# A gated linear attention with a mixture of experts on one core: the opening in another order, the attention's transfers spread over its steps, and the last 64 tokens of an expert in one load of weights

## The chip, the cores and the metric

The kernel runs on one core of one Trainium2 chip. The time is the device time of one execution in microseconds (us). The core has five engines with a queue of instructions each: PE (matrix products; its loads of the stationary operand are listed apart as PEld), DVE (vector work), ACT (activations and copies), POOL (vector work and indirect transfers) and SP, which here only issues transfers. Every engine works its queue in order; semaphores make it wait for the others. Transfers run beside the engines on 16 DMA engines.

## The reference

Two stages follow each other. The first is a gated linear attention for 4 batches, 8 heads, 768 positions and 40 dimensions, whose gates are kept in range by a running maximum `m`; the second sends each of the 3072 rows (4 x 768) of 320 values to one of 8 experts.

```python
for t in range(S):
    kt, vt, qt = (k[:, :, t], v[:, :, t], q[:, :, t])
    m_new = np.maximum(f_gate[:, :, t] + m, i_gate[:, :, t])
    f_stab = np.exp(f_gate[:, :, t] + m - m_new)
    i_stab = np.exp(i_gate[:, :, t] - m_new)
    m = m_new
    C = f_stab[:, :, None, None] * C + i_stab[:, :, None, None] * np.einsum('bhd,bhe->bhde', vt, kt)
    n = f_stab[:, :, None] * n + i_stab[:, :, None] * kt
    h_tilde = np.einsum('bhde,bhe->bhd', C, qt)
    nq = np.einsum('bhd,bhd->bh', n, qt)[:, :, None]
    denom = np.maximum(np.abs(nq), 1.0)
    o = 1.0 / (1.0 + np.exp(-o_gate[:, :, t]))
    y[:, :, t] = o * h_tilde / denom
...
xn = x / (np.linalg.norm(x, axis=-1, keepdims=True) + 1e-06)
en = expert_emb / (np.linalg.norm(expert_emb, axis=-1, keepdims=True) + 1e-06)
logits = xn @ en.T / tau
expert_idx = np.argmax(logits, axis=1)
...
gate_w = probs[np.arange(N), expert_idx]
...
for e in range(E):
    mask = expert_idx == e
    ...
    h = np.maximum(x[mask] @ w1[e], 0.0)
    out[mask] = gate_w[mask, None] * (h @ w2[e])
```

The first weights `w1` of an expert are 320 x 1024, the second ones `w2` 1024 x 320, all in float32.

## The kernel before

**Order.** All engines' orders are written out by hand: the instructions of each engine run as the code issues them (`tc.manual_schedule`), and buffers that come round again make the later user wait.

**Attention.** The loop `for n in range(NS)` makes 24 steps. Step n is one window j of 128 positions of one batch b (`j, b = divmod(n, 4)`), all 8 heads in 4 pairs (a pair lies on partitions 0 to 39 and 64 to 103). A window is worked as two chunks of 64 positions. In a step the code issues, among other things: `stage_add` (the chunk's product of keys and weighted values, tile `c`), `stage_next` and `stage_mid` (the state after a window, `c_st`, and between its chunks, `c_mid`; in the first steps both are ACT copies), `stage_scores(n + 1)` (32 products of queries and keys into `s`), `stage_uv(n + 2)` (POOL: the values times their gate factors, `uv`), `stage_weigh(n + 1)` (DVE: the causal mask on `s`, giving `w_s`), `stage_y(n)` (48 to 64 products into `y`), and, for the steps behind, the denominators, the output gate (`sig`), the rows `x`, their store to `x_d` and the logits of the routing (`route`).

**Opening.** Step 0 has gate factors of its own that are made in a short way (`gates_scan(0)`, `u0`). The factors of all other windows come from `gates_chain`, a generator whose pieces run whenever the code calls `tick`; it ends in three exponentials on ACT (`gu`, `gam`, `gp`) and the DVE matrices `gr`. In step 1 `while vq: tick()` drains what is left of it before the scores of step 2, and `gates_turn` brings its results onto the partitions (PE) and into `u_t`, `e_t` and `g_t`. Ahead of the loop stand the zeroing of the buffers (POOL, DVE and, by `zero_act`, ACT), the two 40 x 40 identities `j40`, and warm-up products (`fill`: 9 at the start, 3 before the first scores).

**Transfers.** SP issues the loads. `stage_rows` (keys and values by position, 2 transfers, 648 KB) and `stage_dims` (keys and queries by dimension, 4 transfers, 640 KB) bring the data of two steps, both in every even step, two pairs ahead. `stage_sig` loads the output gate of 4 steps (640 KB), `stage_store` writes `x` of 4 steps. `W_AT` names the steps in which the weights of the first two experts are loaded, one load for each entry: 512 KB each for the first and second third of `w1`, the rest twice for the last third, and four pieces of `w2`; the list of loads starts at step 9.

**Experts.** The two most chosen experts are worked in two halves ("a" and "b"), the other six one after the other with room for `CAPS` = (448, 448, 384, 384, 320, 320) rows, which are gathered by index (POOL, `xs`). `x_chunk` transposes them on PE and splits them into a high and a low part. `mm1` multiplies with `w1`, also split: 8 products per block f of 128 hidden units; ACT writes the high part `hh` of the result and DVE the low part `hl`. `mm2` then takes up to 128 rows at a time (`TILES`) and sums 24 products (`hh` with both parts of `w2`, `hl` with the high part); with 448 and 320 rows the last tile has 64. DVE multiplies with the routing weight, and POOL writes the rows by index.

Of the kernel before, what the change touches and what calls it, by code (L numbers as in the profile page):

```python
# [50 lines left out]
W_AT = (9, 10, 11, 13, 14, 16, 18, 20, 22)  # L51
# [4 lines left out]
FILLS = (9, 3, 3)  # L56
# [8 lines left out]
def tile_mlstm_moe(  # L65
# [93 lines left out]
    def load_expert(e, at=None):  # L159
# [3 lines left out]
        def load(i):  # L163
            def go():
                raw = raws[i] = wp.tile([P, F], F32, name=f"raw_{e}_{i}", tag="raw", bufs=7)
                if i < 2:
                    SY.dma_start(raw, w1_[i * P : (i + 1) * P])
                elif i == 2:
                    SY.dma_start(raw[0:L], w1_[2 * P : DM])
                    SY.dma_start(raw[L:P], w1_[2 * P : DM])  # L170
# [194 lines left out]
    def mm1(ws, x, xc, f, hs, hc):  # L365
# [10 lines left out]
        V.scalar_tensor_tensor(hl, ph, 0.0, hh.bitcast(F32), ALU.max, ALU.subtract)  # L376
# [4 lines left out]
    def mm2_sum(ws, hs, ts_, nm, mid=None, late=False):  # L381
# [11 lines left out]
        return po  # L393

# [61 lines left out]
    with ExitStack() as actx:  # L456
# [65 lines left out]
        def stage_sig(j):  # L522
            sigs[j] = tp.tile([P, B, DM], F32, name=f"sig_{j}", tag="sig", bufs=2)
            SY.dma_start(sigs[j], og[:, j * B : (j + 1) * B])
# [135 lines left out]
        def stage_store(n):  # L660
            j, b = divmod(n, B)
            if b == B - 1:
                SY.dma_start(xrows(j), xs_[j])
# [313 lines left out]

        fill(FILLS[0])
# [10 lines left out]
        for r in range(2):  # L989
            r0 = r * L  # L990
            V.tensor_copy(j40[r0 : r0 + D], ident[r0 : r0 + D, r0 : r0 + D])
# [50 lines left out]
        for t in (q_s[2], *c_st, ent, xt_s[0][:, 2], xt_s[1][:, 2]):  # L1042
            G.memset(t, 0.0)
# [11 lines left out]
        def gates_chain():  # L1055
# [3 lines left out]
            V.tensor_copy(fp[:, :, 0], gs[:, :, P - 1])  # L1059
            V.tensor_tensor(fp[:, :, 1], last, gs[:, :, P - 1], ALU.add)  # L1060
            yield
            for jj in range(NJ):
                V.tensor_copy(fpj[:, :, :, jj], fp[jj * NH : (jj + 1) * NH].rearrange("p k w -> p w k"))
# [4 lines left out]
            for jj in range(NJ):  # L1068
                V.tensor_copy(mj[jj * NH : (jj + 1) * NH], mm[:, jj : jj + NJ * (NK - 1) + 1 : NJ])
# [96 lines left out]
        for n in range(NS):  # L1166
            last = n == NS - 1
            if n and n % 2 == 0 and n + 4 < NS:
                stage_rows(n // 2 + 2)
                stage_dims(n // 2 + 2)  # L1170
            if n % B == 1 and n // B + 1 < NW:
                stage_sig(n // B + 1)
            if n == W_AT[0]:
                for k in range(NE):
                    exps[k] = load_expert(
                        k, nc.values_load(first[0:1, k : k + 1], engines=[ET.SP], min_val=0, max_val=E - 1)
                    )
                exps[0]["tiles"](wp, 1)
                w_loads = [exps[0]["load"](i) for i in range(7)] + [exps[1]["load"](i) for i in range(2)]
# [21 lines left out]
            if n == 0:  # L1201
                SY.dma_start(en, emb)
                stage_sig(0)
# [48 lines left out]
            if not last:  # L1252
                route(n, 0)
# [201 lines left out]
    for e in range(NE, E):  # L1455
# [17 lines left out]
        for f in range(FC):  # L1473
            mm1(ws, x, w, f, hs, w)
            do(1)
        for a, t in enumerate(TILES[j]):
            mm2(ws, hs, t, gt[0 : t.stop - t.start, a : a + 1], ids_v[j][a], f"{e}_{a}")
            for _ in range(1 + (a == 1)):
# [302 lines left out]
```

## Time and profile before

| what | value |
| --- | --- |
| median of 3 runs | 382.38 us (378.32 to 391.39) |
| time of the profiled execution | 382.01 us |
| its span, first to last instruction | 380.2 us |
| mean granted clock of PE in it | 0.936 |
| busy: PE, PEld, DVE, ACT, POOL | 331.9, 308.3, 225.9, 139.8, 179.5 us |
| moved by DMA | 55.92 MB |

The span is 1.8 us shorter than the execution's time; the rest lies before the first and after the last instruction. Rows of a timeline give start, duration, engine, line of the code, operation, output and inputs, and in brackets how long the engine had been idle and what ended that. "issue" means that the profile shows nothing that it waited for. In a window's row stand length, busy time of the engines with the number of instructions, the clock granted to PE (1.00 is full), the share of time that the DMA engines were busy, and GB/s. Busy times of PE overlap within a pipeline, so that PE is shown busy also where it runs below its best.

### The profile page before, as it was taken

The page shows a single profiled execution, that of the slowest core. Times are in us where ns is not written, and L with a number is a line of the kernel's source. Part 1 is how long each engine was busy: PE and PEld are TensorE (multiplying, and loading weights), DVE is VectorE, ACT ScalarE, POOL GpSimd, SP SyncE. Part 2 cuts the span into 40 slices and gives each one's busy share as a digit, 9 for nine tenths or more (in the row PEclk, how much of TensorE's full clock was granted, in tenths as well). Part 3 has the DMA queues.
Part 4 walks back from the last instruction along what each step waited for, and adds up shares of the span by engine and source line. Part 5 has one row for each costly group of instructions (what it writes and reads, how often), then busy time and mean ns, then how long its engine had stood idle before and what let it go on. Part 6 is the DMA issues. An engine that isn't in the chain of part 4 may idle for free. (4 is left out here: it accounts for less than half of the span.)

```text
span 380.2 us, 10504 instructions
## 1 busy us (share of the span) xinstructions
PE 331.9 (87%) x4163; PEld 308.3 (81%) x4163; DVE 225.9 (59%) x617; ACT 139.8 (37%) x375; POOL 179.5 (47%) x216
## 2 busy tenths in 40 slices
PE   4969999769997799986889989998999999999920
PEld 1759998759986699886789879997999999999920
DVE  8646888567796579952446664473465765864200
ACT  3354332132432366341244363262253543642000
POOL 5718666445674748275615721182252432724120
PEclk8768999898998899999989999998999999999995
DMA  6772969986784352020493847327328456210010
GB/s 189 229 214 93 293 220 316 211 274 186 244 248 161 104 173 76 1 72 0 153 259 109 248 166 175 103 87 194 92 72 257 127 166 180 75 49 13 19 33 1
DMA packets 26604, 55.92 MB, mean 147 GB/s; under 512 B 4209, under 2 KB 16213, under 8 KB 26545
## 3 DMA queue, kind: packets, MB, share of 16 engines
q1 hardware_dynamic: 22688, 46.72, 41.7%
q0 software_dynamic: 3456, 8.16, 6.9%
q8 instruction: 35, 0.57, 0.6%
q10 hardware_dynamic: 400, 0.27, 0.2%
q14 instruction: 25, 0.20, 0.2%
HBM read 47.31 MB, written 8.21 MB: 146 GB/s over the span
## 5 line engine op out<-in xcount | busy, mean ns | idle before, releaser
L407 POOL DMA_INDIRECT out<-ob,ids x20 | 19.8, 992 | 85.8 <-DVE ob L404 70.9
L388 PE MATMUL po<-w2h,hh 128*128 128x320 f32 (+1 forms) x160 | 51.0, 319 | 0.0
L388 PE MATMUL po<-w2h,hl 128*128 128x320 f32 (+1 forms) x160 | 50.2, 314 | 0.0
L388 PE MATMUL po<-w2l,hh 128*128 128x320 f32 (+1 forms) x160 | 50.1, 313 | 0.0
L375 ACT ACTIVATE hh<-ph 128x448 fp32r<-128x448 f32 (+2 forms) x48 | 23.6, 493 | 54.0 <-PE ph L373 49.1
L376 DVE SCALAR_TENSOR_TENSOR hl<-ph,hh 128x448 fp32r<-128x448 f32 (+2 forms) x48 | 26.7, 557 | 24.8 <-ACT hh L375 18.3
L531 POOL TENSOR_TENSOR uv<-vr_s,u_t 64x328 f32<-64x328 f32 x46 | 34.2, 744 | 15.2 <-PE c L581 5.0
L373 PE MATMUL ph<-xh,w1h 128*128 128x448 f32 (+2 forms) x96 | 32.2, 338 | 2.1 <-DVE hl L376 2.1
L659 POOL TENSOR_TENSOR x<-x,sig 128x320 f32<-128x320 f32 x21 | 18.2, 867 | 33.1 <-ACT sig L639 13.0
L624 PE MATMUL y<-uv,w_s 128*64 128x82 f32 x384 | 31.7, 252 | 2.1 <-issue 2.1
L633 PE MATMUL y<-c_mid,q_s 128*64 128x82 f32 x192 | 29.6, 245 | 4.1 <-ACT c_mid L597 4.1
L678 ACT COPY xt_s<-px 128x256 f32<-128x256 f32 x24 | 9.0, 373 | 64.3 <-PE px L676 64.2
L545 PE MATMUL s<-q_s,k_o 128*64 128x64 f32 x384 | 30.4, 239 | 2.2 <-issue 2.2
L404 DVE TENSOR_SCALAR ob<-po,gt 128x320 f32<-128x320 f32 (+1 forms) x20 | 11.0, 549 | 35.8 <-PE po L388 35.7
L373 PE MATMUL ph<-xh,w1l 128*128 128x448 f32 (+2 forms) x96 | 32.0, 335 | 0.0
L545 PE MATMUL s<-q_s,k_e 128*64 128x64 f32 x384 | 30.5, 239 | 0.3 <-DVE w_s L554 0.2
L545 PEld LDWEIGHTS s<-q_s,k_e 128*64 128x64 f32 x384 | 27.6, 153 | 3.8 <-issue 2.4
L388 PEld LDWEIGHTS po<-w2h,hh 128*128 128x128 f32 (+1 forms) x160 | 29.1, 182 | 0.8
L581 PE MATMUL c<-uv,kr_s 128*40 128x41 f32 x704 | 25.4, 213 | 4.7 <-issue 4.7
L388 PEld LDWEIGHTS po<-w2h,hl 128*128 128x128 f32 (+1 forms) x160 | 29.0, 181 | 0.4
L388 PEld LDWEIGHTS po<-w2l,hh 128*128 128x128 f32 (+1 forms) x160 | 28.9, 181 | 0.4
L189 ACT CAST w1h<-raw 128x512 fp32r<-128x512 f32 x48 | 29.0, 614 | 0.0
(312 smaller groups left out, 1007.3 us busy)
## 6 DMA issues: line engine op xcount, KB each, us to landing
raw<-in_w SPq DMA_DIRECT2D x32, 320.0 KB
raw<-in_w SPq DMA_DIRECT2D x16, 512.0 KB
raw<-in_w SPq DMA_DIRECT2D x16, 256.0 KB
sig<-in_og SPq DMA_DIRECT2D x6, 640.0 KB
x_d<-x SPq DMA_DIRECT2D x6, 640.0 KB
vr_s<-in_vr SPq DMA_DIRECT2D x11, 328.0 KB
kr_s<-in_kr SPq DMA_DIRECT2D x11, 320.0 KB
q_s<-in_qt SPq DMA_DIRECT2D x22, 160.0 KB
```

Source lines behind the costliest of these rows:

```text
L189: A.copy(h, src)
L373: T.matmul(ph, lt, rh, start=i == 0, stop=i == len(ops) - 1)
L375: A.activation(hh, ph, AF.Relu)
L376: V.scalar_tensor_tensor(hl, ph, 0.0, hh.bitcast(F32), ALU.max, ALU.subtract)
L388: T.matmul(po[0 : ts_.stop - ts_.start, 0:DM], lt[f][:, ts_], rh[:, f], start=k == 0, stop=k == len(ops) - 1)
L407: G.indirect_dma_start(out=out, out_offset=bass.IndirectOffsetOnAxis(ap=slots, axis=0), in_=ob, in_offset=None, bounds_check=NT - 1, oob_i ...
L531: (eng or G).tensor_tensor(uv[n % NB][rows, :, :, r], vr_s[q % NB][rows, k], u_t[rows, j, b].unsqueeze(3).broadcast_to([L, 2, NP, D1]), AL ...
L545: T.matmul(s[r * L : r * L + L, c, a], kk[q % NB][:, k, a, cs], q_s[q % NB][:, k, a, cs], start=True, stop=True,)
L581: T.matmul(pc[r * L : r * L + D, a], kr_s[q % NB][:, k, c, a], uv[n % NB][:, c, a, r], start=not c, stop=not c or a == NP - 1,)
L624: T.matmul(ya[c], w_s[n % NB][:, c, a], uv[n % NB][:, c, a].rearrange("p r d -> p (r d)"), start=True, stop=n < B and c == 0,)
L633: T.matmul(ya[c], q_s[q % NB][:, k, a, c * L : c * L + L], state[:, a], start=False, stop=True)
L659: (eng or V).tensor_tensor(x, x, sg, ALU.mult)
```

## The change

The change has three parts.

**Opening.** The copies of small tiles on DVE (`j40`, `fp`, `fpj`, `mj`) become maxima of the source with itself (`copy_tt`: one operation with two inputs). `FILLS` goes from (9, 3, 3) to (14, 5). `k_o[2]` is zeroed by POOL in front of `c_st`, where ACT did it in step 0. `route(n, 0)`, which also calls `tick`, is left out in step 0, so that the gate chain's exponentials are issued in step 1. On ACT, where the chain's exponentials (`gu`, `gam`, `gp`) stood between the zeroing of `k_o` and the state copies of steps 0 and 1, the order before is

```order
L597 COPY c_mid_171<-c_302 40x4x41 x2
L958 ACTIVATE k_e_160<-onef 128x1024
L958 ACTIVATE k_o_161<-onef 128x1024
L1074 ACTIVATE gu<-gi,na 96x128 x2
L1078 ACTIVATE gam<-gam 96x2
L1082 ACTIVATE gp<-gp 96x256
L607 COPY c_st_167<-c_302 40x4x41 x2
L597 COPY c_mid_172<-c_394 40x4x41 x2
L639 ACT_TABLE_LOAD
```

and the same place (steps 0 and 1 on ACT) now reads

```order
L624 COPY c_mid_171<-c_310 40x4x41 x2
L984 ACTIVATE k_e_160<-onef 128x1024
L634 COPY c_st_167<-c_310 40x4x41 x2
L624 COPY c_mid_172<-c_390 40x4x41 x2
L1102 ACTIVATE gu<-gi,na 96x128 x2
L1106 ACTIVATE gam<-gam 96x2
L1110 ACTIVATE gp<-gp 96x256
L666 ACT_TABLE_LOAD
```

The copies into `c_st` and into `c_mid` of step 1 moved ahead of the exponentials, and the zeroing of `k_o` is gone from ACT.

**Transfers.** `stage_rows` runs in even steps and `stage_dims` in odd ones. The output gate is loaded one step's share at a time (160 KB, three steps ahead), and `x` is stored in every step. `w1` of the first expert comes in six halves of a third (columns 0 to 511 of all thirds first), in steps 9 to 14; the pieces of `w2` in steps 20 and 21, the next expert's first two in step 22. On SP, in steps 9 to 11, the order before is as follows (`raw` are weights, `ISA` stands ahead of a load whose address comes from a register, `kr_s` and `vr_s` rows, `k_e`, `k_o` and `q_s` dims):

```order
L167 DMA raw_0_1231<-in_w 128x1024
L510 DMA kr_s_156<-in_kr 128x640
L511 DMA vr_s_157<-in_vr 128x656
L517 DMA k_e_153<-in_kt 40x1024
L517 DMA q_s_155<-in_qt 40x1024
L517 DMA k_o_154<-in_kt 40x1024
L517 DMA q_s_155<-in_qt 40x1024
L167 ISA
L167 DMA raw_1_1335<-in_w 128x1024
```

and at the same place now, with a share of the output gate (`sig`) and a store of `x` between them:

```order
L169 DMA raw_0_1254<-in_w 128x512
L536 DMA kr_s_156<-in_kr 128x640
L537 DMA vr_s_157<-in_vr 128x656
L551 DMA sig_1140<-in_og 128x320
L689 DMA x_d<-x_1206 128x320
L169 ISA
L169 DMA raw_1_1356<-in_w 128x512
L543 DMA k_e_153<-in_kt 40x1024
L543 DMA q_s_155<-in_qt 40x1024
L543 DMA k_o_154<-in_kt 40x1024
L543 DMA q_s_155<-in_qt 40x1024
L551 DMA sig_1140<-in_og 128x320
```

The four loads by dimension moved behind the next step's weights, which are half as large, and the gate's shares and a store came in between.

**Last 64 tokens.** Where an expert's rows end in a tile of 64 (448 and 320 rows), `mm1` writes the low part of these 64 columns not into `hl` but behind the high part in `hh`, with a second DVE operation. `mm2_tail` then loads the 128 columns (64 high, 64 low) as one stationary operand and multiplies them with both parts of `w2`, 16 products; ACT copies the lower 64 partitions of the sum, DVE adds the upper ones. (The product of the low parts, which `mm2` left out, is thereby added.) This tile comes second instead of last. On POOL, from the stores of an expert with 448 rows to the gathers of the next one's, the order before is

```order
L407 DMA out<-ob_0_3825,ids 3072x320
L407 DMA out<-ob_1_3866,ids 3072x320
L407 DMA out<-ob_2_3914,ids 3072x320
L407 DMA out<-ob_3_3948,ids 3072x320
L312 DMA gt_3953<-gate_d,ids 128x1 x3
L312 DMA gt_3953<-gate_d,ids 64x1
L291 DMA xs<-x_d,ids 128x320 x3
```

and now

```order
L433 DMA out<-ob_0_3880,ids 3072x320
L433 DMA out<-ob_3_3913,ids 3072x320
L433 DMA out<-ob_1_3963,ids 3072x320
L433 DMA out<-ob_2_3997,ids 3072x320
L314 DMA gt_4002<-gate_d,ids 128x1 x3
L314 DMA gt_4002<-gate_d,ids 64x1
L293 DMA xs<-x_d,ids 128x320 x3
```

The store of the 64-row tile (number 3) moved to second place; the gathers behind the stores are the same.

The diff, cut where lines only repeat what is said above:

```diff
-W_AT = (9, 10, 11, 13, 14, 16, 18, 20, 22)
+W_AT = (9, 10, 11, 12, 13, 14, 20, 20, 21, 21, 22, 22)
-FILLS = (9, 3, 3)
+FILLS = (14, 5)
...
-        def load(i):
+        def load(i, half=None):
             def go():
-                raw = raws[i] = wp.tile([P, F], F32, name=f"raw_{e}_{i}", tag="raw", bufs=7)
+                if not half:
+                    raws[i] = wp.tile([P, F], F32, name=f"raw_{e}_{i}", tag="raw", bufs=7)
+                raw, f = raws[i], slice(0, F) if half is None else slice(half * 512, half * 512 + 512)
...
-    def mm1(ws, x, xc, f, hs, hc):
+    def mm1(ws, x, xc, f, hs, hc, tail=False):
...
-        V.scalar_tensor_tensor(hl, ph, 0.0, hh.bitcast(F32), ALU.max, ALU.subtract)
+        n = hc.stop - hc.start
+        m = n - L if tail else n
+        V.scalar_tensor_tensor(hl[:, 0:m], ph[:, 0:m], 0.0, hh[:, 0:m].bitcast(F32), ALU.max, ALU.subtract)
+        if tail:
+            V.scalar_tensor_tensor(
+                hs[0][f][:, n : n + L], ph[:, m:n], 0.0, hh[:, m:n].bitcast(F32), ALU.max, ALU.subtract
+            )
+    def mm2_tail(ws, hs, ts_, gate, slots, nm):
+        w2h, w2l, hh = ws["w2h"], ws["w2l"], hs[0]
+        po = pp[0].tile([P, 512], F32, name=f"po_{nm}", tag="po")
+        for f in range(FC):
+            for w in (w2h, w2l):
+                T.matmul(
+                    po[:, 0:DM],
+                    hh[f][:, ts_.start : ts_.start + P],
+                    w[:, f],
+                    start=f == 0 and w is w2h,
+                    stop=f == FC - 1 and w is w2l,
+                )
+        ob = mp.tile([P, DM], F32, name=f"ob_{nm}", tag="ob", bufs=3)[0:L]
+        A.copy(ob, po[L:P, 0:DM])
+        V.tensor_tensor(ob, po[0:L, 0:DM], ob, ALU.add)
+        mm2_out(None, gate, slots, nm, ob)
...
-        def stage_sig(j):
-            sigs[j] = tp.tile([P, B, DM], F32, name=f"sig_{j}", tag="sig", bufs=2)
-            SY.dma_start(sigs[j], og[:, j * B : (j + 1) * B])
+        def stage_sig(j, b):
+            if b == 0:
+                sigs[j] = tp.tile([P, B, DM], F32, name=f"sig_{j}", tag="sig", bufs=2)
+            SY.dma_start(sigs[j][:, b], og[:, j * B + b])
...
-            if b == B - 1:
-                SY.dma_start(xrows(j), xs_[j])
+            SY.dma_start(xrows(j)[:, b], xs_[j][:, b])
...
+        def copy_tt(dst, src):
+            V.tensor_tensor(dst, src, src, ALU.max)
...
-            V.tensor_copy(j40[r0 : r0 + D], ident[r0 : r0 + D, r0 : r0 + D])
+            copy_tt(j40[r * L : r * L + D], ident[r * L : r * L + D, r * L : r * L + D])
...
-        for t in (q_s[2], *c_st, ent, xt_s[0][:, 2], xt_s[1][:, 2]):
+        for t in (q_s[2], k_o[2], *c_st, ent, xt_s[0][:, 2], xt_s[1][:, 2]):
             G.memset(t, 0.0)
...
-            if n and n % 2 == 0 and n + 4 < NS:
-                stage_rows(n // 2 + 2)
-                stage_dims(n // 2 + 2)
-            if n % B == 1 and n // B + 1 < NW:
-                stage_sig(n // B + 1)
+            if n and n // 2 + 2 < NS // 2:
+                (stage_dims if n % 2 else stage_rows)(n // 2 + 2)
+            if n and n + B - 1 < NS:
+                stage_sig(*divmod(n + B - 1, B))
...
-                zero_act(k_o[2])
                 stage_rows(2)
-                stage_dims(2)
...
-            if not last:
+            if n and not last:
                 route(n, 0)
...
-            mm1(ws, x, w, f, hs, w)
+            mm1(ws, x, w, f, hs, w, CAPS[j] % P == L)
...
+        order_ = list(range(len(TILES[j])))
+        if CAPS[j] % P == L:
+            order_.insert(1, order_.pop())
```

More of the change, by code (lines that the diff above doesn't have):

```diff
@@ L161, in load_expert @@
         w1_, w2_ = (w[e] if at is None else w[ds(at, 1)].rearrange("o p f -> (o p) f") for w in (w1, w2))
-        def load(i):
+        def load(i, half=None):
             def go():
-                raw = raws[i] = wp.tile([P, F], F32, name=f"raw_{e}_{i}", tag="raw", bufs=7)
+                if not half:
+                    raws[i] = wp.tile([P, F], F32, name=f"raw_{e}_{i}", tag="raw", bufs=7)
+                raw, f = raws[i], slice(0, F) if half is None else slice(half * 512, half * 512 + 512)
                 if i < 2:
-                    SY.dma_start(raw, w1_[i * P : (i + 1) * P])
+                    SY.dma_start(raw[:, f], w1_[i * P : (i + 1) * P, f])
                 elif i == 2:
-                    SY.dma_start(raw[0:L], w1_[2 * P : DM])
-                    SY.dma_start(raw[L:P], w1_[2 * P : DM])
+                    SY.dma_start(raw[0:L, f], w1_[2 * P : DM, f])
+                    SY.dma_start(raw[L:P, f], w1_[2 * P : DM, f])
                 else:
@@ L1058, in gates_chain @@
             last = gp[:, :, P - 1]
-            V.tensor_copy(fp[:, :, 0], gs[:, :, P - 1])
+            copy_tt(fp[:, :, 0], gs[:, :, P - 1])
             V.tensor_tensor(fp[:, :, 1], last, gs[:, :, P - 1], ALU.add)
@@ L1062, in gates_chain @@
             for jj in range(NJ):
-                V.tensor_copy(fpj[:, :, :, jj], fp[jj * NH : (jj + 1) * NH].rearrange("p k w -> p w k"))
+                copy_tt(fpj[:, :, :, jj], fp[jj * NH : (jj + 1) * NH].rearrange("p k w -> p w k"))
             V.memset(mm[:, 0:1], -1e30)
@@ L1068, in gates_chain @@
             for jj in range(NJ):
-                V.tensor_copy(mj[jj * NH : (jj + 1) * NH], mm[:, jj : jj + NJ * (NK - 1) + 1 : NJ])
+                copy_tt(mj[jj * NH : (jj + 1) * NH], mm[:, jj : jj + NJ * (NK - 1) + 1 : NJ])
             yield
@@ L1178, in tile_mlstm_moe @@
                 exps[0]["tiles"](wp, 1)
-                w_loads = [exps[0]["load"](i) for i in range(7)] + [exps[1]["load"](i) for i in range(2)]
+                w_loads = [exps[0]["load"](*p) for p in PIECES1] + [exps[0]["load"](i) for i in range(3, 7)]
+                w_loads += [exps[1]["load"](i) for i in range(2)]
             stage_add(n, 0)
@@ L1202, in tile_mlstm_moe @@
                 SY.dma_start(en, emb)
-                stage_sig(0)
+                for b in range(B):
+                    stage_sig(0, b)
             if n == 3:
@@ L1473, in tile_mlstm_moe @@
         for f in range(FC):
-            mm1(ws, x, w, f, hs, w)
+            mm1(ws, x, w, f, hs, w, CAPS[j] % P == L)
             do(1)
-        for a, t in enumerate(TILES[j]):
-            mm2(ws, hs, t, gt[0 : t.stop - t.start, a : a + 1], ids_v[j][a], f"{e}_{a}")
-            for _ in range(1 + (a == 1)):
+        order_ = list(range(len(TILES[j])))
+        if CAPS[j] % P == L:
+            order_.insert(1, order_.pop())
+        for i, a in enumerate(order_):
+            t = TILES[j][a]
+            r = t.stop - t.start
+            (mm2_tail if r == L else mm2)(ws, hs, t, gt[0:r, a : a + 1], ids_v[j][a], f"{e}_{a}")
+            for _ in range(1 + (i == 1)):
                 if xps:
```

1 line of the change is left out of this document (removed).

## The prediction

> **What bounds the kernel now.** I read the page's totals first, then the engines' busy time by stage, then PE's idle gaps in the timeline, then the DMA view of the same stretches. From the page, the span and the queue that carries instructions:
>
> ```profile
> span 380.2 us, 10504 instructions
> ...
> q8 instruction: 35, 0.57, 0.6%
> ```
>
> The stages (stretch, length, busy time of PE, PE's weight loads, DVE, ACT and POOL with their instructions, clock, DMA share, GB/s); from the second to the fifth they begin where the scores of a step begin:
>
> ```profile
> 0.00:28.35 28.35, 18.47 (x280) 14.03 (x282) 17.52 (x51) 11.62 (x27) 13.99 (x33) 0.75 0.71 209
> 28.35:61.61 33.26, 33.26 (x904) 30.46 (x900) 26.10 (x98) 12.84 (x48) 23.32 (x40) 0.96 0.67 214
> 61.61:92.20 30.59, 24.57 (x598) 22.22 (x594) 18.96 (x71) 7.77 (x27) 16.89 (x21) 0.89 0.87 255
> 92.20:108.72 16.52, 16.52 (x479) 15.13 (x475) 13.80 (x51) 6.42 (x22) 10.89 (x13) 1.00 0.74 246
> 108.72:123.96 15.24, 12.95 (x322) 11.46 (x318) 11.47 (x39) 4.92 (x17) 8.86 (x12) 0.89 0.59 170
> ```
>
> PE is busy without a break in the second and fourth stretch and loses time in the first, third and fifth. The scores alone (32 matmuls a step) give the pace:
>
> ```profile
> 33.59:61.61 28.02, 8.02 (x224) 7.29 (x226) 1.00 0.69 221
> 61.61:92.20 30.59, 7.45 (x160) 6.95 (x162) 0.89 0.87 255
> 108.72:123.96 15.24, 3.61 (x96) 3.13 (x98) 0.89 0.59 170
> ```
>
> Seven steps in 28.02 us are 4.00 a step; five in 30.59 are 6.12; three in 15.24 are 5.08. In the slow steps PE stops and no other engine ends the stop ("issue"):
>
> ```profile
> 71.59 0.29 PE L624 MATMUL y<-uv,w_s 128*64 128x82 f32 x2 [2.08 <-issue]
> ...
> 116.07 0.22 PE L545 MATMUL s<-q_s,k_o 128*64 128x64 f32 x1 [2.21 <-issue]
> ```
>
> From stop to stop PE runs about 128 matmuls and 127 weight loads; below, such a block without a stop, then the two about the stop at 71.59:
>
> ```profile
> 41.46:45.75 4.29, 4.29 (x139) 3.98 (x133) 3.24 (x10) 1.35 (x5) 2.66 (x4) 1.00 0.97 297
> 64.72:71.59 6.87, 4.79 (x128) 4.28 (x127) 3.53 (x15) 1.86 (x6) 4.89 (x6) 1.00 1.01 256
> 71.59:78.75 7.16, 6.31 (x127) 5.80 (x127) 4.27 (x17) 1.35 (x5) 2.43 (x4) 0.76 0.83 211
> ```
>
> The page's 0.57 MB in 35 packets are 16 KB each, and the stops lie 255 instructions apart: I read them as the edges of blocks of code. In the DMA view the stretch from 64.72 to 68.5 holds data alone (the first fence is its one queue), and the next code packet comes between 68.5 and 71.6:
>
> ```profile
> q1 hardware_dynamic: 392, 1.06, 95.8%
> ```
>
> ```profile
> q8 instruction: 1, 0.02, 2.6%
> ```
>
> So the next block of code waits about 4 us behind full data queues, and what PE runs through in 4.29 us takes 7. In the opening PE waits for a data chain (below); in the experts it is nearly always busy.
>
> **The change, part by part.** (1) Opening. DVE's rows (the copies to j40; a two-input operation, twice; the gate chain's first and last steps), the spread of the two copies, then POOL's rows:
>
> ```profile
> 2.42 3.53 DVE L991 COPY j<-ident 40x40 f32<-40x40 f32 x2
> ...
> 7.60 0.29 DVE L1009 TENSOR_TENSOR gi<-gi,gs 96x128 f32<-96x128 f32 x1
> ...
> 16.35 0.29 DVE L1009 TENSOR_TENSOR gi<-gi,gs 96x128 f32<-96x128 f32 x1
> ...
> 17.12 0.64 DVE L1060 TENSOR_TENSOR fp<-gp,gs 96x2 f32<-96x2 f32 x1
> ...
> 21.28 0.35 DVE L1088 TENSOR_TENSOR gr<-ident,gam 96x192 f32<-96x192 f32 x1
> ```
>
> ```profile
> L991 DVE COPY j<-ident x2: 182/1757/3332, 2.4 to 5.8; 40x40 f32<-40x40 f32 x2
> ```
>
> ```profile
> 5.07 0.64 POOL L997 MEMSET uv<- 128x656 f32 x1
> ...
> 14.01 0.95 POOL L1043 MEMSET q_s<- 128x1024 f32 x1
> 14.89 1.31 POOL L1043 MEMSET c_st<- 128x328 f32 x4
> ...
> 16.20 0.35 POOL L1043 MEMSET xt_s<- 128x128 f32 x2
> 16.99 1.56 POOL L531 TENSOR_TENSOR uv<-vr_s,u_t 64x328 f32<-64x328 f32 x2 [0.44 <-PE c L581]
> ```
>
> One copy took 3.33 us, the other 0.18; the long one ends when POOL's last memset does (5.71). A two-input operation took 0.29 beside POOL's memsets (16.35, with xt_s at 16.20) as it did with POOL idle (7.60), so as maxima the two cost about 2 x 0.18 and DVE comes 3.2 us earlier to the gates, if their rows have landed by then; bounds 0 and 3.2, taken 2.7, near the upper end since the gate rows are issued first of all. The seven later copies may gain or lose: L1060, two inputs on 2 columns, took 0.64 beside POOL's uv at 16.99, more than 128 columns at 16.35, but the chain now runs earlier, beside memsets. I count 0, bounds -0.5 and +1.6 (the length of both uv).
>
> The Trainium skill ("SBUF — State Buffer", Who interferes with whom) says that a VectorE instruction with two SBUF inputs contends with a GpSimd instruction that reads SBUF, not with one that only writes. The rows at 16.35 and 17.12 agree; by that rule the maxima lose at most the same 1.6, should uv come alongside.
>
> The exponentials move behind the middle state of step 1 on ACT:
>
> ```profile
> 19.92 0.69 ACT L1074 ACTIVATE gu<-gi,na 96x128 f32<-96x128 f32 x2 [3.38 <-DVE na L1072]
> ...
> 21.86 0.60 ACT L597 COPY c_mid<-c 40x164 f32<-40x164 f32 x2
> ```
>
> ```profile
> 22.51 0.40 PE L633 MATMUL y<-c_mid,q_s 128*64 128x82 f32 x1 [4.13 <-ACT c_mid L597]
> ```
>
> What is late next is POOL: its memset of k_o (0.95, as q_s's) now stands ahead of c_st, whose first quarter then ends at 14.89 + 0.95 + 1.31/4 = 16.2; ACT copies c_st and c_mid, 0.6 each, and y of step 1 starts at 17.4 instead of 22.51: 5.1 us. From there to 28.35 lie 5.84 us at a low clock (0.75 over the stretch); without PE's stop I take a quarter off, 1.4. Term 1: -6.5. Its ends: -4 (the gate chain's last row, gr, stays at 21.6 and holds the matrices that turn the gates) and -8.5 (POOL is 2 us earlier as well). The warm-up matmuls (five more at the start, two more before the first scores) lie under the wait for DVE and POOL; without that cover the two cost 1.0:
>
> ```profile
> 9.88 1.47 PE L949 MATMUL warm<-ones 128*128 128x512 bf16 x3
> ```
>
> (2) Transfers. Every step now issues one share of sig and one store, rows and dims alternate, and the first weights come as six halves over steps 9 to 14, the second weights in steps 20 and 21. The bytes of a pair of steps stay; what falls is the heap at a time: rows, dims and 0.5 MB of weights in one step before, rows or dims and 0.25 MB now.
>
> ```profile
> 17.61 0.35 SPq L524 DMA_DIRECT2D sig<-in_og  x1
> ```
>
> At such an issue every 0.4 us the fullest step, with nine, keeps SP 3.6 of 4.0 us. The store waits for POOL's product of that step, and behind it stand loads that are needed two steps later: 0. Steps 10 to 14 without stops: 598 matmuls at 33.26/904 are 22.0 us, less the routing's small ones, so I take 4.25 a step, 21.2, instead of 30.59: -9.4. But their DMA time was 0.87 x 30.59 = 26.6 us, and less 0.66 MB of second weights and half of the first load it is some 21: nearly full at that pace. I give back 0.5 a step, 2.4. Term 2: -7.0, ends -1 and -9.4. Steps 20 to 22: three at 4.25 are 12.75 instead of 15.24; a rest of 1.0 stays for the weights moved there. Term 3: -1.5, ends +1 and -2.5.
>
> (3) Last 64 tokens. DVE's rows for the first product of an expert (count, busy, mean ns), the 24 matmuls of one 64-row tile, a wait for gathered rows, and the last three stores on POOL:
>
> ```profile
> L376 DVE SCALAR_TENSOR_TENSOR hl<-ph,hh 128x448 fp32r<-128x448 f32 x16 | 10.0, 623 | 8.6 <-ACT hh L375 6.9 <-issue 1.6
> L376 DVE SCALAR_TENSOR_TENSOR hl<-ph,hh 128x384 fp32r<-128x384 f32 x16 | 8.9, 556 | 9.0 <-ACT hh L375 5.8 <-issue 3.2
> ```
>
> ```profile
> 240.85:244.30 3.45, 3.45 (x26) 3.12 (x24) 1.00 0.46 104
> ```
>
> ```profile
> 262.96 0.33 PE L336 MATMUL pt<-ident,xs 128*128 128x128 f32 x1 [1.07 <-DMA xs<-x_d,ids]
> ```
>
> ```profile
> 357.82 1.04 POOL L407 DMA_INDIRECT out<-ob,ids  x1 [8.04 <-DVE ob L404]
> 363.48 1.00 POOL L407 DMA_INDIRECT out<-ob,ids  x1 [4.61 <-issue]
> 366.77 0.92 POOL L407 DMA_INDIRECT out<-ob,ids  x1 [2.29 <-DMA out<-ob,ids]
> ```
>
> Eight of 24 matmuls go in each of four experts: 3.45/24 x 8 = 1.15 us, 4.6 in all. The split of hl makes two DVE operations of one: 64 columns are worth 0.623 - 0.556 = 0.07, so of 0.556 six times that is length and 0.15 is paid for every operation; 32 more operations are some 5 us of DVE beside PE, which is free there half of the time (8.6 and 9.0 us of idle time ahead of 10.0 and 8.9 of work). Expert 2's share is lost where expert 3 waits for gathered rows (262.96), since POOL's stores before that gather are as many; the last one's may be lost, since its stores start 3 to 6 us apart. Two count in full, -2.3, the other two at 0.35 each. Term 4: -3.0, ends -0.5 (DVE late) and -4.6.
>
> The sum: -6.5 - 7.0 - 1.5 - 3.0 = -18.0. The profiled execution took 382.0 (380.2 and 1.8 around it), 0.4 under the median of 382.38: 364.0.
>
> **The rivals.** *Code waits as before.* The bytes are the same, so terms 2 and 3 are 0: 382.0 - 9.5 = 372.5. For it: stretch two had shares of 0.67 to 0.69 without stops, and even 0.97 in the block at 41.46, so share alone does not decide; against it: the two blocks about the stop at 71.59 stood at 1.01 and 0.83 (only the stop at 116.07 lies in a stretch of 0.59). The Trainium skill ("Runtime: NRT & Kernel Launch", Instruction fetch mechanics) holds that crossing a 16 KiB block is mostly hidden; by that rule PE's stops are something else and this rival's 372.5 stands; the code packet that comes only after 68.5 speaks against it.
> *The opening keeps its length*, because DMA (0.71 there) or gr holds it: term 1 is -1: 369.5.
> *DVE bounds the experts*: its 5 us come onto the path where the columns are fewest, 320: term 4 is +3: 370.
> *Slower.* With transfers in every step no gap is left for code: each of some 16 blocks from 28 to 92 and 108 to 124 us takes 7 us instead of 4.3, also the 11 that ran free: +2.7 x 11 = +30 against -9.5: 402. It decides once a code packet waits over 1.9 us in the plain steps too; there the share was 0.69 with the same bytes, which speaks against it.
>
> **How the numbers follow.** Chances: the forecast 0.64 (own range 356 to 371), code waits 0.15, opening kept 0.09, DVE 0.05, slower 0.05, something else 0.02. The range takes in the two next rivals and, with the ends of all terms partly together (-6 and -28), runs from 354 to 376. A measurement tells about 2% (7.6 us) from no change: faster means under 374.4. That is nearly all of the forecast and most of three rivals at their centre: 0.84; within 2%: 0.10; slower 0.06.
>
> **What would show it.** Right: the copies' successors at 0.2 us each and the gates begun before 5 us; y of step 1 before 19 us with c_mid ahead of gu on ACT; scores of step 3 near 22; steps 10 to 14 at under 4.8 us, no PE stop over 1 us to "issue" there; 16 matmuls in 2.3 us per last tile. Wrong: PE stops of 2 us still at every 255th instruction, the scores of step 3 after 26, or hl delaying PE in the first product.

## The result, and the profile after

The changed kernel took 370.22 us (median of 4 runs, 369.43 to 371.31) against 381.55 us for the kernel before (4 runs, one more than ahead of the prediction, 378.32 to 391.39). The ratio is 0.9722 with a 95% interval of 0.9657 to 0.9788: faster. Medians and ranges are of all runs, ratios of those alone that lie near the fastest of their kernel, and where no ratio is given, too few of these were left. Its profiled execution took 369.50 us, with a span of 367.7 us.

The same five stretches as in the prediction, now of the changed kernel (stretch, length, busy time of PE, PEld, DVE, ACT and POOL, clock, DMA share, GB/s); they begin again with the scores of steps 3, 11, 16 and 20:

```profile
0.00:22.60 22.60, 17.01 (x287) 12.65 (x289) 14.85 (x51) 10.39 (x24) 14.47 (x33) 0.92 0.75 225
22.60:57.53 34.93, 33.02 (x906) 29.89 (x902) 26.35 (x98) 13.05 (x50) 23.35 (x40) 1.00 0.73 223
57.53:82.46 24.93, 21.54 (x598) 19.42 (x594) 20.55 (x71) 7.77 (x27) 16.72 (x21) 1.00 0.88 263
82.46:98.99 16.53, 16.53 (x479) 15.14 (x475) 13.81 (x51) 6.42 (x22) 10.87 (x13) 1.00 0.83 245
98.99:111.62 12.63, 11.72 (x322) 10.43 (x316) 12.07 (x40) 5.07 (x17) 8.77 (x12) 1.00 0.62 163
```

The opening is 5.8 us shorter, the third stretch 5.7 and the fifth 2.6; the second is 1.7 longer, and there PE is no longer busy all the time. What follows is the end of the attention, up to the first product of an expert, in the kernel before and (second fence) after:

```profile
123.97:134.77 10.80, 8.63 (x158) 7.35 (x152) 6.43 (x20) 3.90 (x15) 7.04 (x8) 0.84 0.39 112
```

```profile
111.63:125.07 13.44, 10.19 (x148) 8.56 (x148) 6.59 (x22) 3.75 (x14) 7.15 (x8) 0.68 0.82 268
125.07:367.70 242.63, 213.09 (x1440) 203.40 (x1438) 134.03 (x324) 94.03 (x226) 97.97 (x93) 0.96 0.38 110
```

That end is 2.6 us longer, with the DMA share at 0.82 where it was 0.39; the rest (second line) took 380.20 - 134.77 = 245.4 us before and 242.6 now. The sum of the seven differences is the 12.5 us between the two spans. In that end PE waits once for gathered rows, as it did not before:

```profile
121.31 0.90 PE L353 MATMUL pa<-ident,xs_a 128*128 128x128 f32 x3 [1.13 <-DMA xs_a<-x_d,ids_a]
```

In the opening, the timeline of the changed kernel has the two small identities on DVE at once, the last step of the gate chain at 18.52, and, in the second fence, the state copies on ACT ahead of the exponential:

```profile
2.42 0.40 DVE L1005 TENSOR_TENSOR j<-ident 40x40 f32<-40x40 f32 x2
...
18.52 0.90 DVE L1116 TENSOR_TENSOR gr<-ident,gam 96x192 f32<-96x192 f32 x1
```

```profile
16.16 0.60 ACT L634 COPY c_st<-c 40x164 f32<-40x164 f32 x2 [5.24 <-POOL c_st L1071]
16.77 0.59 ACT L624 COPY c_mid<-c 40x164 f32<-40x164 f32 x2
17.39 0.69 ACT L1102 ACTIVATE gu<-gi,na 96x128 f32<-96x128 f32 x2
```

c_mid of step 1 stood at 21.86 before and stands at 16.77. PE's largest waits of the opening are now transfers (rows of PE, with the idle time ahead and what ended it):

```profile
11.00 0.24 PE L572 MATMUL s<-q_s,k_e 128*64 128x64 f32 x1 [1.86 <-DMA q_s<-in_qt]
...
16.58 0.24 PE L572 MATMUL s<-q_s,k_e 128*64 128x64 f32 x1 [2.40 <-DMA sig<-in_og]
```

The scores read keys and queries and not the gate; the gate's load, which the second row names, is the one that the profile saw land last (in other runs q_s or k_o stands there).

PE's stops at the edges of code blocks have become shorter but are not gone; the three longest between the scores of step 3 and those of step 23:

```profile
41.12 0.27 PE L572 MATMUL s<-q_s,k_o 128*64 128x64 f32 x1 [1.11 <-issue]
...
75.94 0.39 PE L608 MATMUL c<-uv,kr_s 128*40 128x41 f32 x10 [1.00 <-issue]
81.60 0.27 PE L887 MATMUL pm<-oa,op 128*128 128x32 f16 x4 [1.12 <-issue]
```

The block ahead of the stop at 75.94 shows the same sight as before: from 69.1 to 73.2 the DMA view has one queue (first fence), and the packet of code comes between 73.2 and 75.9.

```profile
q1 hardware_dynamic: 665, 1.14, 102.5%
```

```profile
q8 instruction: 1, 0.02, 2.4%
```

In the experts DVE does the low part in two operations (first fence: the low part of the whole tiles and of the last 64 columns), and PE waits for gathered rows in the expert with 384 rows that follows the two of 448 (they are the rows of the next one):

```profile
L380 DVE SCALAR_TENSOR_TENSOR hl<-ph,hh 128x384 fp32r<-128x384 f32 x32 | 17.8, 555 | 18.2 <-ACT hh L377 12.1 <-issue 6.0
L382 DVE SCALAR_TENSOR_TENSOR hh<-ph,hh 128x64 fp32r<-128x64 f32 x32 | 6.8, 213 | 0.0
```

```profile
277.49 0.33 PE L338 MATMUL pt<-ident,xs 128*128 128x128 f32 x1 [0.96 <-DMA xs<-x_d,ids]
...
279.13 0.33 PE L338 MATMUL pt<-ident,xs 128*128 128x128 f32 x1 [1.31 <-DMA xs<-x_d,ids]
```

### The profile page after: what moved, and what is told of

Read it like the earlier page. It is cut to its first block, busy times and chain, and to the rows that moved or that the text cites. A ratio compares the mean times of both kernels' runs of the same rounds, so it can differ in the third digit from the quotient of the medians.

```text
span 367.7 us, 10594 instructions
## 1 busy us (share of the span) xinstructions
PE 323.1 (88%) x4138; PEld 299.5 (81%) x4138; DVE 228.3 (62%) x653; ACT 140.5 (38%) x378; POOL 179.3 (49%) x217
## 5 line engine op out<-in xcount | busy, mean ns | idle before, releaser
L377 ACT ACTIVATE hh<-ph 128x448 fp32r<-128x448 f32 (+2 forms) x48 | 23.6, 492 | 54.4 <-PE ph L375 37.7
L396 PE MATMUL po<-w2h,hh 128*128 128x320 f32 x128 | 40.9, 319 | 0.0
L396 PE MATMUL po<-w2h,hl 128*128 128x320 f32 x128 | 40.3, 315 | 0.0
L396 PE MATMUL po<-w2l,hh 128*128 128x320 f32 x128 | 40.3, 314 | 0.0
L380 DVE SCALAR_TENSOR_TENSOR hl<-ph,hh 128x384 fp32r<-128x384 f32 (+1 forms) x48 | 24.5, 511 | 25.2 <-ACT hh L377 16.1
L572 PE MATMUL s<-q_s,k_e 128*64 128x64 f32 x384 | 27.4, 224 | 5.5 <-DMA sig<-in_og 2.4
L686 POOL TENSOR_TENSOR x<-x,sig 128x320 f32<-128x320 f32 x21 | 18.2, 865 | 26.3 <-DVE x L685 11.2
L572 PEld LDWEIGHTS s<-q_s,k_e 128*64 128x64 f32 x384 | 24.4, 138 | 6.6 <-issue 3.0
L194 DVE TENSOR_TENSOR w2l<-raw,w2h 128x320 fp32r<-128x320 f32 x58 | 27.1, 503 | 0.2
L651 PEld LDWEIGHTS y<-uv,w_s 128*64 128x64 f32 x384 | 22.3, 143 | 4.5 <-issue 4.5
L572 PEld LDWEIGHTS s<-q_s,k_o 128*64 128x64 f32 x384 | 24.5, 138 | 1.5 <-issue 1.5
L608 PE MATMUL c<-uv,kr_s 128*40 128x41 f32 x704 | 23.8, 206 | 1.9 <-issue 1.9
L191 ACT CAST w2h<-raw 128x320 fp32r<-128x320 f32 x62 | 25.2, 460 | 0.0
```

The source lines that it names most:

```text
L191: A.copy(h, src)
L194: (eng or V).tensor_tensor(lo, src, h.bitcast(F32), ALU.subtract)
L377: A.activation(hh, ph, AF.Relu)
L380: V.scalar_tensor_tensor(hl[:, 0:m], ph[:, 0:m], 0.0, hh[:, 0:m].bitcast(F32), ALU.max, ALU.subtract)
L396: T.matmul(po[0 : ts_.stop - ts_.start, 0:DM], lt[f][:, ts_], rh[:, f], start=k == 0, stop=k == len(ops) - 1)
L572: T.matmul(s[r * L : r * L + L, c, a], kk[q % NB][:, k, a, cs], q_s[q % NB][:, k, a, cs], start=True, stop=True,)
```

## The experiments

The experiments ran in three groups, each on one chip beside the kernel before: its median was 385.20 us in the first group (35 runs), 369.17 in the second (17) and 382.13 in the third (7). Totals are therefore compared within a group.

**The three parts, each alone, and more loads early.** The first kernel has only the opening's edits, the second only those of the transfers, the third only those of the last 64 tokens; each edit is the part of the diff above.

> Part alone: only the opening is changed (maxima, fills, zeroing of k_o[2], place of the exponentials); transfers and experts as before. Theory: the whole step of the changed kernel, scores of step 3 at 22.6 instead of 28.4, comes from the opening and stays: -5.8 us, ratio 0.985. Rival: a part of it came from the transfers (fewer loads by dimension in step 0), so only -3 to -4 us, scores of step 3 at 24 to 25.

Measured: 385.99 us (12 runs), ratio 1.005, interval 0.9974 to 1.0126: no gain is shown. The scores of step 3 came at 22.14, as expected, but those of step 4 only at 30.67 (before 33.60). ACT's row and then PE's row:

```profile
24.26 0.47 ACT L639 ACTIVATE sig<-sig 128x320 f32<-128x320 f32 x1 [4.56 <-DMA sig<-in_og]
```

```profile
25.77 0.33 PE L674 MATMUL px<-ident,x 128*128 128x128 f32 x1 [2.51 <-POOL x L659]
```

The output gate's 640 KB are issued behind the rows and dims of step 0, and ACT waits for them with the copies of u_t behind it. Half of what the opening gained goes there at once; both theories had the place of step 3 in mind and neither this wait. Steps 10 to 14 took 30.0 us, as before. Steps 15 to 19 took 19.1 us where the profile before has 16.5, with stops of 0.94 and 1.19 at edges of code, and steps 20 to 22 took 12.4 instead of 15.2.

> Part alone: only the transfers are changed. Theory (code waits behind bulk loads): steps 10 to 14 fall from 30.6 to about 25 us and steps 20 to 22 by 2.6, while steps 3 to 9 lose 1.7 to new stops and the end of the attention loses up to 2.6 at the gathers; net -4 to -7 us, ratio 0.982 to 0.99. Rival: the end of the attention's loss is not from the transfers: net -7 to -8.

Measured: 380.85 us (12 runs), ratio 0.9929 (0.9861 to 0.9996), 2.7 us less; the size is below both theories' ranges, though the interval reaches into that of the first. Steps 10 to 14 did what was expected (24.3 us), steps 20 to 22 became 1.2 us shorter and not 2.6 (14.0). Steps 3 to 10 took 34.05, as they do in the next kernel, which has the old transfers (34.07), and the end of the attention took 10.25, no more than before: alone, this part does not lengthen it.

> Part alone: only the last 64 tokens are changed. Theory (the four 1.17 us are gained, and one expert gives back some 4 us because a gather collides with loads of weights that come earlier): between -0.5 and -2 us. Rival: the tile's shortening stays and the delay of the gather in the changed kernel is chance: -4 to -5 us, ratio 0.988.

Measured: 380.38 us (12 runs), ratio 0.9925 (0.9856 to 0.9993): 2.9 us, between the two, and the interval holds both. Each of the four tiles' products is 1.1 to 1.2 us shorter (the second product of the first expert of 448 rows took 16.1 us before and 15.0 here, that of the first one of 320 rows 12.2 and 11.1). This kernel runs the attention of the kernel before instruction by instruction, so it is also a second draw of it. Its steps 10 to 14:

```profile
61.10:88.23 27.13, 22.88 (x598) 20.76 (x594) 19.67 (x71) 7.77 (x27) 15.41 (x20) 0.94 0.92 275
```

27.13 us where the profile before shows 30.59, and the scores of step 23 at 118.66 instead of 123.97: 5.3 us between two executions of the same instructions up to there.

The fourth kernel of the group adds loads that nobody reads:

```diff
+            if n in (4, 5, 6, 7):
+                load_expert(0)["load"](0)()
             if n in W1_AT:
```

> The kernel before with four more loads of 512 KB (rows of the first expert's first weights that nobody reads) issued at the ends of steps 4, 5, 6 and 7, where PE ran without a stop. Theory (blocks of code wait behind full data queues): PE stops of 1 to 2.5 us to 'issue' appear in three or four blocks between 45 and 65 us; +4 to +8 us. Rival (the stops of steps 10 to 14 have another cause, such as the pieces of the weights or the loads by register): no such stop, within +1 us.

Measured: 386.88 us (10 runs), ratio 0.9998 (0.9874 to 1.0123). The interval of 1.2% either way leaves the total open. Two stops follow the loads, which SP issues between 39.6 and 49.3 us:

```profile
49.24 0.22 PE L545 MATMUL s<-q_s,k_e 128*64 128x64 f32 x1 [0.88 <-issue]
```

```profile
54.91 0.33 PE L674 MATMUL px<-ident,x 128*128 128x128 f32 x1 [0.91 <-issue]
```

The third kernel, without these loads, has stops of 0.47 and 0.45 at 44.5 and 49.5. The expected size fell: half a megabyte more in a step went with some 0.4 us more at a stop there, not 1 to 2.5, and steps 10 to 14 of this execution (25.5 us) are the shortest of all with the old loads. That the stops belong to code blocks follows from something else. In the 14 profiles of this study PE stopped to "issue" for over 0.25 us 61 times between 28 and 112 us. Within each profile these stops lie 256 PE instructions apart or a multiple of that, within two instructions, and PE goes on 2.2 to 3.1 us after a packet of the instruction queue has begun. With 16 or 17 such blocks in each profile about one edge in four stops PE. What tells these edges from the others is how late the packet comes, counted from PE's entry into the block before. At the 61 edges with a stop it began 2.1 to 6.4 us after that entry; at the 169 others it began within 2.7 us in all but two cases, with a median of 1.3. In the first 2 us after the entry the DMA engines were busy with data for 0.89 of the time ahead of a stop and for 0.73 otherwise, on average, and the two groups overlap. So a late packet stands at every stop; that the data make it late is likely, but no run shows it by itself.

**Parts together.** The first kernel is the opening with only the gate's load by steps:

```diff
-            if n % B == 1 and n // B + 1 < NW:
-                stage_sig(n // B + 1)
+            if n and n + B - 1 < NS:
+                stage_sig(*divmod(n + B - 1, B))
```

The second has the opening and all of the transfers, the fourth is the changed kernel with the edit just shown undone. The third is the changed kernel with two groups of gathers exchanged:

```diff
-        if j:
-            gt = gather_gates(e, ids_v[j])
         if e + 1 < E:
...
             xs = gather(ids_v[j + 1]) if j else xs_n
...
             do(7)
+        if j:
+            gt = gather_gates(e, ids_v[j])
```

> The opening alone plus one part of the transfers: the output gate comes one step's share at a time. Theory (the opening's gain was given back because the first product with the gate waits for a load of 640 KB): PE's wait for x near 25.8 us goes, scores of step 4 at 26.5 to 27.5 instead of 30.7, and about 4 us less than the opening alone, ratio 0.985 to 0.993. Rival (rows and dims in one step hold the opening as well): scores of step 4 still after 29, ratio 1.0.

Measured: median 369.97 us (12 runs, 359.25 to 374.44) against 369.17 for the kernel before: no gain in the medians, and no ratio with runs that far apart. PE's wait for x at 25.8 is gone, and from the scores of step 3 to those of step 4 it took 4.5 us instead of 8.5. The scores of step 4 still came only at 28.3 instead of 30.7, since those of step 3 stood at 23.8; steps 10 to 14 took 30.3 us with the old loads.

> Opening and transfers together, experts as before. Theory (the opening needs the shares of the gate, the parts multiply otherwise): the changed kernel without its last tiles, 0.972 / 0.9925, ratio 0.979, attention's last scores near 112 us. Rival (the parts only add): 1.005 x 0.993, ratio 0.998, last scores near 116.

Measured: 367.61 us (6 runs), ratio 0.9896 (0.9803 to 0.9989). The attention did what the theory said (scores of step 23 at 110.40), the total lies between the two, with an interval that holds the rival's 0.998 and just not the theory's 0.979. In this execution the second products of the second and the third of the six later experts, beside which the next expert's rows are gathered, took 20.2 and 15.8 us (18.7 and 11.9 in the profile before), 5.4 us of it given back there.

> The changed kernel with the gathers of the next expert's rows issued ahead of those of this expert's routing weights. Theory (two experts wait for rows whose gathers end behind the weights' loads, 1.5 and 2.3 us, and the second loses clock after it): rows are asked for 3.9 us earlier, both waits go, 3 to 5 us less than the changed kernel, ratio 0.960 to 0.964. Rival (the routing weights, now later, hold the first tile's output, or DMA is late anyway): 0 to 1 us, ratio 0.97 to 0.972.

Measured: 352.12 us (6 runs), ratio 0.9574 (0.9513 to 0.9635). PE no longer waits for gathered rows in the six later experts (earlier it still does, 4.3 us for xs_a). The stretch from the first second product to the next expert's first product, in the expert of 384 rows with the two waits above, for the changed kernel and then for this one:

```profile
272.56:288.52 15.96, 13.69 (x82) 13.07 (x82) 6.28 (x13) 5.06 (x13) 2.10 (x3) 0.89 0.52 142
```

```profile
260.79:272.34 11.55, 11.55 (x82) 11.53 (x82) 5.76 (x12) 4.32 (x11) 2.23 (x3) 1.00 0.60 171
```

Same 82 products, 4.4 us less, and the clock stays at 1.00. On the same chip, in the kernel with the opening and the transfers, the second products of the second and the third later expert took 20.2 and 15.8 us; here they took 13.9 and 11.6, and 1.2 us of the difference belong to the new last tile. In these stretches the gain is larger than expected. This version is faster than the kernel before. Its interval also lies below that of the changed kernel (0.9657 to 0.9788), which was measured on another chip; the kernel nearest to it on this chip is the next one, with 360.40 us.

> The changed kernel with one thing undone: the output gate is loaded for four steps at a time, 640 KB, as before. Theory: the wait for x near 25.8 us is back, scores of step 4 at 30 to 31 instead of 26.7, +4 to +6 us, ratio 0.983 to 0.988. Rival (rows and dims apart free the queues early enough): under +1.5 us, ratio 0.972 to 0.976.

Measured: 360.40 us (6 runs), ratio 0.9758 (0.9692 to 0.9824). The theory fell in its place: the scores of step 4 came at 25.0, earlier than in the changed kernel. With the dims moved to the next step the gate's load stands ahead of them in SP's queue and is in time; either move would have done. From the scores of step 3 to those of step 4 it took 4.3 us here, 4.5 in the kernel with shares alone, and 8.5 with neither. Steps 3 to 10 of this execution took 38.6 us instead of 34.9, with stops of 0.84 and 2.48 at edges of code; it was the longest of the six runs, so that the gate's load costs anything there is not shown.

**One thing undone at a time.** All four kernels are the changed one; the first has its copies back (the same for j40, fpj and mj):

```diff
-            copy_tt(fp[:, :, 0], gs[:, :, P - 1])
+            V.tensor_copy(fp[:, :, 0], gs[:, :, P - 1])
```

> The changed kernel with one thing undone: the small tiles are copied with copies again, not as maxima. Theory (POOL's row of memsets in front of c_st sets when the second step's product starts, so what DVE gains before it is not on the path): scores of step 0 up to 3 us later, scores of step 3 within 0.7 us of the changed kernel's 22.6, total within 1 us of it. Rival (the forecast's 2.7 us for the copies are on the path): scores of step 3 near 25.3, +2.7 us.

Measured: median 374.54 us (4 runs, 368.86 to 377.68) against 371.81 for the changed kernel in the same group (365.50 to 376.18); runs that far apart leave the total open. The scores of step 0 came at 10.82, 3.1 us later than there, and those of step 3 at 23.54, against 23.27: in this the theory held. ACT's rows:

```profile
16.79 0.60 ACT L634 COPY c_st<-c 40x164 f32<-40x164 f32 x2 [1.65 <-POOL c_st L1069]
17.40 0.59 ACT L624 COPY c_mid<-c 40x164 f32<-40x164 f32 x2
20.15 0.69 ACT L1100 ACTIVATE gu<-gi,na 96x128 f32<-96x128 f32 x2 [2.15 <-DVE na L1098]
```

The gate chain is late again (gu at 20.15) but holds nothing that PE needs at once.

The second issues the gate chain's rest in step 0 again:

```diff
-            if n and not last:
+            if not last:
                 route(n, 0)
```

> The changed kernel with one thing undone: the gate chain's exponentials are issued in step 0 again, ahead of the state copies of step 1 on ACT. Theory (this order is what held step 1): the first product with c_mid starts 2 to 4 us later, scores of step 3 at 25 to 27 instead of 22.6, total +3 to +4 us. Rival (DVE's gate chain ends early enough now that the order no longer matters): scores of step 3 within 1 us, total the same.

Measured: median 371.84 us (4 runs, 368.48 to 375.17), against 371.81 for the changed kernel; scores of step 3 at 23.76. The theory fell. ACT's rows show why:

```profile
15.84 0.69 ACT L1102 ACTIVATE gu<-gi,na 96x128 f32<-96x128 f32 x2 [4.70 <-DVE gam L1104]
...
17.38 0.59 ACT L634 COPY c_st<-c 40x164 f32<-40x164 f32 x2
17.98 0.59 ACT L624 COPY c_mid<-c 40x164 f32<-40x164 f32 x2
```

With the maxima the gate chain is ready 4 us earlier than before (gu at 19.92), so the exponentials are done when POOL has zeroed c_st. Maxima and order are two ways to the same gain: with one of them the scores of step 3 came at 23.5 and 23.8, inside the range of the kernels that have both (20.7 to 23.9), where the old opening has 27.0 to 28.5. In both runs PE waits for keys and queries, until 16.8 and 17.7. The warm-up products and the place where k_o is zeroed stayed new in both, and no run undoes maxima and order together.

The third has the old table of the weights' loads, and loads them whole:

```diff
-W_AT = (9, 10, 11, 12, 13, 14, 20, 20, 21, 21, 22, 22)
+W_AT = (9, 10, 11, 13, 14, 16, 18, 20, 22)
...
-                w_loads = [exps[0]["load"](*p) for p in PIECES1] + [exps[0]["load"](i) for i in range(3, 7)]
-                w_loads += [exps[1]["load"](i) for i in range(2)]
+                w_loads = [exps[0]["load"](i) for i in range(7)] + [exps[1]["load"](i) for i in range(2)]
```

> The changed kernel with one thing undone: the first two experts' weights are loaded whole and in the steps of before (9, 10, 11, 13, 14, 16, 18, 20, 22). Theory (the heap of bytes ahead of a block of code makes PE's stops): steps 10 to 14 take 25 to 28 us instead of 22 to 23.5, with stops over 1 us, and the end of the attention is 2 us shorter again (10 to 11 instead of 12.3 to 13.4), total +1 to +3 us. Rival (rows and dims in separate steps are what helps): steps 10 to 14 within 1 us of 23, total -1 to -2 us.

Measured: median 369.03 us (4 runs, 367.11 to 375.43), not more than the changed kernel's 371.81. Steps 10 to 14, of this kernel and then of the changed one in the same group:

```profile
57.42:84.36 26.94, 21.55 (x600) 19.44 (x594) 19.81 (x71) 7.77 (x27) 17.56 (x22) 1.00 0.94 274
```

```profile
57.72:81.42 23.70, 21.54 (x598) 19.42 (x594) 20.48 (x71) 7.77 (x27) 16.82 (x22) 1.00 0.91 265
```

This execution took 3.2 us more there, within what was expected and 1.0 more than the longest of the eight with the new transfers (23.5 to 25.9); the end of the attention took 10.9 us, 0.7 less. Both are single executions, and the total shows no loss with four runs of such spread.

The fourth is the changed kernel itself.

> The changed kernel once more, as the base for the three above on one chip. Theory: ratio 0.972 again within 0.006, steps 10 to 14 in 22 to 23.5 us, the gathered rows of two experts waited for. Rival (its first comparison was a favourable draw, the sum of the parts alone is 0.99): ratio over 0.98.

Measured: 371.81 against 382.13 us, a quotient of 0.973 of the medians (4 and 7 runs). The fastest runs of the two, 365.50 and 371.92 us, give 0.983. By both the kernel is the faster one again, but the size is not settled, and this group does not rule out the rival's 0.98. Steps 10 to 14 took 23.7 us. Of the two waits for gathered rows only the first came (1.2 us); the second product of the third later expert took 12.2 us here, 16.0 in the first profile of the same kernel.

## Why the forecast came out as it did

The measured 370.22 us lies in the range, and the kernel is faster, as forecast; but 11.3 us were gained and not 18. The total alone does not tell the forecast from its rivals (372.5, 369.5 and 370 are nearer to it than 364.0); the stretches do. By stretches (the forecast's terms; the difference of the two profiles; and the means over several profiles: for the opening four that keep the old one and eight with the whole new one, below it five with the old transfers and eight with the new):

| stretch | forecast | the two profiles | means, old to new |
| --- | --- | --- | --- |
| opening, to the scores of step 3 | -6.5 | -5.8 | 27.8 to 22.7 |
| steps 3 to 10 | 0 | +1.7 | 35.1 to 35.1 |
| steps 10 to 14 (scores 11 to 16) | -7.0 | -5.7 | 28.7 to 24.5 |
| steps 20 to 22 | -1.5 | -2.6 | 14.2 to 12.8 |
| end of the attention | 0 | +2.6 | 10.2 to 11.9 |
| experts and rest | -3.0 | -2.8 | |

The two profiles fall 5.5 us short of the forecast, and 4.3 of these lie in two stretches that the sum put at nothing: steps 3 to 10, which the means do not confirm, and the end of the attention, which they do with 1.7. The low end of the stated range, 28 us less, is more than the ends of the four terms together, 25.0. The parts do not simply add: alone they multiply to 0.990 (1.005, 0.9929 and 0.9925), and the whole has 0.972; the first of them loses its gain again where the gate's load is late. On the second chip the first two together stood at 0.990, so how much the parts help each other differs with the chip or the execution.

*Opening.* The size was nearly right, the reason half. The prediction took the order on ACT for the cause and the copies for something that POOL's memsets swallow. POOL was as late as worked out (ACT's copy of c_st waits for it until 16.16; 16.2 was forecast). But the runs with one of the two undone show that either one gives the gain, and PE itself waits at that time for a transfer, until 16.58. That the gain stays depended on something the prediction had put under transfers: the opening alone loses half of it to the gate's 640 KB. The low clock did go, 0.75 to 0.92. The Trainium skill's rule on two-input operations ("SBUF — State Buffer", Who interferes with whom) agrees with gr, which took 0.90 us beside POOL's product uv and 0.35 in the profile before, with POOL idle. PE did not wait for it.

*Steps 10 to 14.* The mechanism is borne out as far as late packets of code go (what delays them is not shown by itself); the size was taken from one execution. The profile before had 30.6 us there, the other executions with the old loads 25.5 to 30.3; the forecast's 21.2 plus 2.4 is 23.6, and the new kernels took 23.5 to 25.9. So the target was nearly met, and the start was an unlucky draw: by the means the term is -4.2. "Under 4.8 us" a step and "no PE stop over 1 us" did not come true (4.99; 1.00 and 1.12). Stops were 6.0 us of the stretch in the profile before and 2.4 in the one after: the 0.5 us a step that was given back is what they still cost. Whether the smaller weights or the rows and dims in separate steps did more is open: the kernel with whole loads lies between old and new. By the Trainium skill's rule that crossing a block is mostly hidden ("Runtime: NRT & Kernel Launch", Instruction fetch mechanics) the rival of 372.5 would have held; three edges in four do pass without a stop here, but the fourth makes those 6.0 us.

*Steps 20 to 22 and the end of the attention.* Here a step of the prediction failed: it left a rest of 1.0 us "for the weights moved there" in steps 20 to 22 and put the end of the attention at nothing. In the seven profiles that have the new transfers behind the new opening (three of them with one edit undone) steps 20 to 22 took 12.6 or 12.7 us, without a stop at an edge of code. The old transfers took 12.4 and 12.6 us in two executions and 15.2 to 15.8 in three, with one stop of 2.2 to 2.6: the gain is a stop that comes in some executions and not in others. Behind these steps 1.7 us are lost in the means. In the changed kernel 1.1 us is the wait for xs_a, and the clock over that end is 0.68 where it was 0.84. But the lengths do not follow the waits: the end took 13.4 us with a wait of 1.1, 12.5 with 4.3 (gathers exchanged), 11.6 with 0.5 (repeated run) and 11.2 with none (exponentials in step 0). The six loads that the gathers now run beside are a likely cause, as 10.9 us with the old loads suggests. They are not shown to be it: the transfers alone took 10.25 us, and the opening with the gate's shares, which has the old loads, waits 1.3 us for xs_a. The cause of this loss stays open.

*Experts.* The term was right in sum, in part by luck. The products are 1.17 us shorter in each of the four experts. Where a loss was feared, at the third expert's rows, PE waits 1.5 us (1.6 before), yet that second product took 15.9 us instead of 18.7. The split of hl cost DVE 0.213 x 32 = 6.8 us for 64 columns less in 32 others, some 2.2: 4.6 net against the 5 forecast. It hardly bounded the six later experts: in their first products PE waits 1.4 us for DVE in the profile after and 2.1 in the one before (0 to 5.7 and 0.2 to 4.8 over all profiles with and without the new tile); 0.4 of the 1.4 lie in the first expert with 320 rows, where a bound was feared. What was lost lies in the next expert, 4.1 us: its rows came 2.3 us late, and the clock was 0.89 there. Kernels without the new tile show the same (15.8 us in the opening with the transfers), and the repeated run of the changed kernel does not (12.2), so it is a collision that both versions can have.

## What to carry to other kernels

Take a stretch with stops from several executions before pricing its repair; two executions of the same instructions differed by 3.5 us in five steps here. When two edits remove the same wait, undo each from the finished kernel before crediting either, and look for what a shorter opening meets next in the load queue. A gather that is needed soon belongs ahead of one that is needed later: with that exchange the ratio was 0.957, where the changed kernel has 0.972 on another chip and, on the same chip, the changed kernel with the gate's load undone has 0.976.

## What the runs showed of the hardware

A copy on DVE beside POOL's memsets took 3.33 us where two maxima of the same tiles took 0.40 together. Three more of these maxima (fpj, at 14.75 in the changed kernel) took 0.48 together beside POOL's memsets of q_s and k_o, which lasted from 13.98 to 15.82.

The execution time of the kernel before varied between 377 and 391 us on one chip, and between 369 and 385 in the medians of the chips. A part of that is not in the attention: in the profile before, ACT waits twice and long in the first products of the shared experts, and the profile names no instruction of this core as the end of these waits ("remote"; waits of ACT between 173 and 197 us: total, times, longest):

```profile
ACT hh_b L375 <- remote: 8.6, 2, 5.2
```

On the chip of the second group that stretch, the first products of the shared experts' second halves, took 14.5 us in all four kernels, in all other profiles 22 to 27. What delays ACT there was not tried, and stays open.
